# Row transposes of the next tile behind three products of the second gemm, beside those of the second relu half; the sum of the logits three products later

## The chip, the cores and the metric

One core of one Trainium2 chip runs the kernel. The metric is device time in microseconds (us). Before the change the median of three runs is 907.2 us (906.87 to 910.54).

## The reference

Causal attention with a retrieval memory (4 batches, 8 heads, 576 positions, width 64) gives 2304 token rows of 512 numbers. Two mixture-of-experts layers follow, 8 experts each, every token going to one expert only:

```python
logits = x @ w_gate                      # layer 1; layer 0 uses normalized rows
expert_idx = np.argmax(logits, axis=1)
for e in range(E):
    mask = expert_idx == e
    h = np.maximum(x[mask] @ w1[e], 0.0)      # 512 -> 1024
    out[mask] = gate_w[mask, None] * (h @ w2[e])   # 1024 -> 512
```

Everything is float32. The kernel keeps that precision by splitting each operand into a high and a low part (fp32r), so that each float32 product is three matrix products: high times high, high times low, low times high.

## The kernel before, in words

Up to about 270 us the attention runs, then layer 0 and layer 1. Tokens are sorted by expert into tiles of 128 rows. A layer is a row of tiles, `step(L, t)` (L1374), with t the tile's number in the layer. The change concerns t=1 to t=21 of both layers; t=0 has code of its own.

One tile on TensorE (PE): **gemm 0** makes two halves of the hidden activations, 12 products into `ph0` and 12 into `ph1`. Each half goes through a relu on ScalarE (ACT, L1392 and L1413), then four 128x128 transposes on PE into `pt0` or `pt1` (`hT`, L1362), then `hilo`: ACT copies the high part (L1193), VectorE (DVE) subtracts to give the low part (L1194). **gemm 1** makes 24 products into `py`, here called q0 to q23, three to each 128-deep block. q0 and q1 read the high part of the first half; q2 is the first product that reads its low part, and q12 the first that reads the second half. The first half's transposes stand among the products of `ph1`, the second half's between q2 and q3.

The rows of the next tile have been gathered by then (`xg`); four transposes (`xT_pe`, L1189) bring them into `psx`, and another `hilo` makes `b.x` of them. In layer 0, four small transposed products with the second layer's gate weights (`parts_pe`, L1292) are copied out by `parts_ev` (DVE, L1295), and one more product (`logits_pe`, L1299) adds the four parts up to the logits of the tile finished before. DVE then routes: `iov` (L1312), `mn`, `t8s`, `km`, `oh` (L1319 to L1323), later `ea`, `sg`, `xcb` (L1327 to L1332). The matrix `oh` feeds `rank_pe` (L1335) in the next tile.

Weights are shared by the tiles of one expert. Where a new expert is coming, each 128x1024 chunk of its weights is split by ACT (L922, high) and by DVE (L925, low); these stand behind runtime branches (`splits`, L1261) at fixed places of each tile, and run only in the tiles that need them: chunk 2 of gemm 0's weights (`splits(0, (2,))`) around the second half's `hilo`, chunk 3 behind the routing up to `oh`, the other chunks behind it and in the next tile. The words that hold the branch flags are loaded in `next_step`. Each engine works through its own queue in the order in which the code writes it, so the order of these lines is the order of the work.

Of the kernel before, what the change touches and what calls it, by code (L numbers as in the profile page):

```python
# [409 lines left out]
def tile_kernel(ctx, tc, q, k, v, M_prev, z_prev, beta, emb, tau, w1a, w2a, wg, w1b, w2b, out):  # L410
# [190 lines left out]
    def place(c0, n):  # L601
        for _ in place_(c0, n):
            pass

    class Route1:
# [32 lines left out]
        def rank_pe(self, ps):  # L638
            n, mm = self.n, nc.tensor.matmul
            self.ps = ps[:, 0:n * E].rearrange("p (n e) -> p n e", e=E)  # L640
            mm(ps[:, 0:n * E], tri, self.o.rearrange("p n e -> p (n e)"), start=True, stop=False)
            mm(self.ps, ones, acc.unsqueeze(1).to_broadcast([P, n, E]), start=False, stop=(n == 1))
            for i in range(n - 1):
                mm(self.ps[:, i + 1:], ones, self.o[:, i:i + 1].to_broadcast([P, n - 1 - i, E]), start=False, stop=(i == n - 2))
# [22 lines left out]
        def rank_ev(self):  # L667
            V = nc.vector
            V.tensor_tensor(out=self.t8, in0=self.o, in1=self.ps, op=ALU.mult)
            yield  # L670
            V.tensor_reduce(out=rkb[:, self.sl], in_=self.t8, axis=AX.X, op=ALU.add)
            yield
# [254 lines left out]
    def split_chunk(c, wv):  # L927
        return [split_hi(c, wv), split_lo(c, wv)]
# [7 lines left out]
    def cp(e, out, in_):  # L936
        if e:
            nc.scalar.activation(out=out, in_=in_, func=AF.Copy)
        else:
            nc.vector.tensor_copy(out, in_)  # L940

    class Hooks:
# [125 lines left out]
        def parts_pe(self, b, ps):  # L1068


            self.ps["lp"] = ps
            g = KD * E
            for n in range(KD):
                nc.tensor.matmul(ps[g * n:g * n + g], enT.rearrange("p k e -> p (k e)"), self.xT[b][:, n, 0:512], start=True, stop=True)

        def parts_ev(self, b):
            cp(1, self.xT[b][:, 0, 0:512], self.ps["lp"])
# [75 lines left out]
    def rows_of(t):  # L1153

        return xgt[t % 2] if t else xg0
# [5 lines left out]
    def drain(g):  # L1161
        for _ in g:
            pass
# [11 lines left out]
    psx, pm1, ph1, pt0, pt1, py, pm0, ph0 = (psp.tile([P, 512], F32, name=x) for x in ("psx", "pm1", "ph1", "pt0", "pt1", "py", "pm0", "ph0"))  # L1175
# [11 lines left out]
    def xT_pe(x):  # L1187
        for kk in range(KD):
            nc.tensor.transpose(psx[:, P * kk:P * kk + P], x[:, P * kk:P * kk + P], ident)  # L1189

    def hilo(ps, hl):
        hi, lo = hl
        nc.scalar.activation(out=hi, in_=ps, func=AF.Copy)  # L1193
        nc.vector.tensor_tensor(out=lo, in0=ps, in1=hi.bitcast(F32), op=ALU.subtract)  # L1194
# [91 lines left out]
    pts = (pt0, pt1)  # L1286
# [10 lines left out]
    def logits_pe(yT):  # L1297

        nc.tensor.matmul(pm1[:, 0:E], yT[:, 0:P], sel, start=True, stop=True)  # L1299

    def yT_pe():
        for kk in range(KD):
            nc.tensor.transpose(pm0[:, P * kk:P * kk + P], ysb[:, P * kk:P * kk + P], ident)

    def yT_ev(yT):
        nc.scalar.activation(out=yT, in_=pm0, func=AF.Copy)
# [4 lines left out]
    def route2_iov():  # L1311
        nc.vector.tensor_scalar(out=rs_["iov"], in0=ioer, scalar1=xcb[:, 2:3], scalar2=None, op0=ALU.mult)  # L1312
# [30 lines left out]
    def begin(L, t):  # L1343

        if t:
            nc.gpsimd.tensor_copy(xca[t % 2], rows_of(t)[:, DM:XR])  # L1346
        if 1 < t < NS - 2:
            gather(L, t + 2)

    def end(L, t):  # L1350
        xc = xca[t % 2] if t else xg0[:, DM:XR]
        nc.scalar.activation(out=ysb, in_=py, func=AF.Copy, scale=xc[:, 0:1])  # L1352
        if L == 0:
            nc.gpsimd.tensor_copy(xcb, xc)
            nc.gpsimd.dma_start(out=x2[P * t:P * t + P, 0:DM], in_=ysb)
        else:
            nc.gpsimd.indirect_dma_start(out=out, out_offset=bass.IndirectOffsetOnAxis(ap=xc[:, 1:2].bitcast(I32), axis=0), in_=ysb, in_offset=None,  # L1357
                                         bounds_check=NTOK - 1, oob_is_err=False)

    def hT(i, b):  # L1360
        for kk in range(4):
            nc.tensor.transpose(pts[i][:, P * kk:P * kk + P], b.hs[i][:, P * kk:P * kk + P], ident)  # L1362
        hilo(pts[i], b.h[i])

    def next_rows(t):
# [3 lines left out]
    def next_step(L, t):  # L1369
        n = steps[L, t] = Step(L, t)  # L1370
        if t > 2:
            n.flags()

    def step(L, t):  # L1374

        s, b = steps[L, t], bufs
        more = 0 < t < NS - 1
        split2 = t > 2
        rt2 = L == 0
        late = t >= NT1 - 2  # L1380
        x = x0 if t == 0 else b.x
        lx = lambda kk: (*x, P * kk)
        lh = lambda kk: (*b.h[kk // 4], P * (kk % 4))
        begin(L, t)
        s.gemm(0, ph0, lx, 0, 0, 3)
        yield
        s.gemm(0, ph0, lx, 0, 3, 9)
        yield
        s.gemm(0, ph0, lx, 0, 9, 12)
        if split2:  # L1390
            s.splits(0, (0, 1))
        nc.scalar.activation(out=b.hs[0], in_=ph0, func=AF.Relu)  # L1392
        if split2:
            s.splits(1, (0,))

        ahead = (L, t) != (0, NT1 - 1)
        if ahead and split2:
            s.loads(0, (0, 1))
            s.loads(1, (0,))
        yield  # L1400
        s.gemm(0, ph1, lx, 512, 0, 6)
        hT(0, b)
        if rt2:
            yT_pe()
            yT_ev(b.hs[0])
        yield
        rk = L == 0 and 2 <= t <= NT1 - 2
        if rk:
            rank_pe(t - 2)
            rank_ev(t - 2)  # L1410
        s.gemm(0, ph1, lx, 512, 6, 12)
        last_mm[0] = s.lm[1]
        nc.scalar.activation(out=b.hs[1], in_=ph1, func=AF.Relu)  # L1413
        yield
        if more:
            xT_pe(rows_of(t + 1))
        if rt2:
            parts_pe(b.hs[0])
            parts_ev(b.hs[0])
        if more:  # L1420
            hilo(psx, b.x)
        if rt2:
            route2_iov()
        s.gemm(1, py, lh, 0, 0, 3)
        if split2:
            s.splits(0, (2,), "h")
        hT(1, b)
        if split2:
            s.splits(0, (2,), "l")
        if more:  # L1430
            next_step(L, t + 1)
        yield
        s.gemm(1, py, lh, 0, 3, 6)
        cs = (1, 2, 3)
        if t == NE:
            s.splits(1, cs)
            cs = ()
        gen = iter(())
        if rt2:
            logits_pe(b.hs[0])  # L1440
        yield
        s.gemm(1, py, lh, 0, 6, 9)
        if rt2:
            gen = route2(t - 1)
        next(gen, None)
        next(gen, None)
        if split2:
            s.splits(0, (3,))
        if split2 and cs:
            s.splits(1, cs)  # L1450
        if t == 2:
            s.flags()
            s.splits(0, range(4))
            s.loads(0, range(4))
        if not ahead:
            e2.append(nc.values_load(ini[0:1, 1, 0:1], engines=[SP_], min_val=0, max_val=E - 1))
            s.loads(0, (0, 1))
            s.loads(1, (0,))
        if split2:
            s.loads(0, (2, 3))  # L1460
            s.loads(1, (1, 2, 3))
        drain(gen)
        if rk and ((t - 1) % 6 == 0 or t == NT1 - 2):
            c0 = (t - 2) // 6 * 6
            place(c0, t - 1 - c0)
        for q_ in range(9, 24, 3):
            yield
            s.gemm(1, py, lh, 0, q_, q_ + 3)
        last_mm[1] = s.lm[1]
        if (L, t) == (1, NT1 - 2):  # L1470

            nc.gpsimd.drain()
        if rt2:
            nc.gpsimd.dma_start(out=x2[P * (t - 1):P * t, DM:XR], in_=xcb)  # L1474
            if late:
                rank_pe(t - 1)
                rank_ev(t - 1)
                place(t - 1, 1)
        if not ahead:

            with tc.If(rg["nt"] <= NT1):
                for c in range(8):
                    for ins in split_chunk(c, rg["wv"]):
                        tc.add_to_no_dep_group("n18", ins)
        end(L, t)
# [71 lines left out]
    b = Bufs(lambda i: Wh[0][:, 1, 512 * i:512 * i + 512] if i < 6 else None)  # L1557
    s = steps[0, 0] = Step(0, 0)
    lx = lambda kk: (*b.x, P * kk)
    lh = lambda kk: (*b.h[kk // 4], P * (kk % 4))  # L1560
# [39 lines left out]
    nc.scalar.activation(out=b.hs[1], in_=ph1, func=AF.Relu)  # L1600
    lo(4)
    hT(0, b)
    hT(1, b)
    run(C, 5)
# [42 lines left out]
    s, b, c = steps[1, 0], bufs, NS - 1  # L1647
    lx = lambda kk: (*x0, P * kk)
    lh = lambda kk: (*b.h[kk // 4], P * (kk % 4))
# [105 lines left out]
```

## Time and profile before

| | before |
|---|---|
| runs, us | 910.54, 906.87, 907.2 (median 907.2) |
| profiled execution, us | 905.06 |
| its span, first to last instruction, us | 903.2 |
| mean granted TensorE clock | 0.991 |
| busy: PE, DVE, ACT, us | 870.2, 502.1, 483.8 |

The profiled execution is 2.1 us below the median of the runs. Times in the rows are counted from the start of its span.

### The profile page before, as it was taken

What the parts mean: (1) busy time and instruction counts of PE and PEld (TensorE: products, weight loads), DVE (VectorE), ACT (ScalarE), POOL (GpSimd) and SP (SyncE); (2) the same over time, 40 slices, a digit from 0 to 9 for tenths busy, and PEclk for the clock granted to TensorE, in tenths of its full rate; (3) what the DMA queues carried; (4) which work ended last, traced back from release to release, by engine and by line L of the source; (5) the groups of instructions that cost most, each with busy time, mean ns of one, the idle gap of its engine ahead of it and who ended that gap; (6) DMA issues with size and microseconds to landing.
All of it is one profiled execution on the core that took longest, in us unless ns stands there. A gap on an engine that the chain in (4) does not pass through costs nothing. (4 is left out here: it accounts for less than half of the span.)

```text
span 903.2 us, 20913 instructions
## 1 busy us (share of the span) xinstructions
PE 870.2 (96%) x5347; PEld 686.9 (76%) x5347; DVE 502.1 (56%) x1585; ACT 483.8 (54%) x972; POOL 275.3 (30%) x375
## 2 busy tenths in 40 slices
PE   6999999999989999998999999998999999999996
PEld 4777777677667777786888877886868888888885
DVE  4655656565684676379535666643567314463430
ACT  3657666666756735376435554532367435564531
POOL 5557635543633011212122312121231212321221
PEclk9999999999999999999999999998999999999998
DMA  7322352411333155359515317111668514384111
GB/s 130 80 52 82 73 170 78 101 40 41 100 111 113 59 211 175 108 165 314 177 49 164 108 37 235 38 49 40 234 203 297 171 48 139 130 305 135 43 38 39
DMA packets 102438, 110.32 MB, mean 122 GB/s; under 512 B 69882, under 2 KB 69882, under 8 KB 102276
## 3 DMA queue, kind: packets, MB, share of 16 engines
q1 hardware_dynamic: 94244, 85.33, 31.1%
q0 software_dynamic: 8032, 23.22, 7.8%
q8 instruction: 54, 0.88, 0.4%
q14 instruction: 108, 0.88, 0.3%
HBM read 90.32 MB, written 19.25 MB: 121 GB/s over the span
## 5 line engine op out<-in xcount | busy, mean ns | idle before, releaser
L1250 PE MATMUL py<-Wh,b 128*128 (+1 forms) x688 | 240.8, 406 | 2.6 <-DVE b L1194 2.4
L1250 PE MATMUL ph<-Wh,b 128*128 (+1 forms) x672 | 226.7, 398 | 0.5 <-ACTq L1261 0.5
L925 DVE TENSOR_TENSOR Wl<-stg,Wh 128x1024 f32 (+1 forms) x120 | 145.5, 1224 | 79.8 <-ACT Wh L922 74.4
L1250 PEld LDWEIGHTS py<-Wh,b 128*128 128x128 f32 x688 | 129.3, 188 | 32.6 <-issue 5.3
L1250 PEld LDWEIGHTS ph<-Wh,b 128*128 128x128 f32 x672 | 126.1, 188 | 26.7 <-ACTq L1261 0.9
L922 ACT ACTIVATE Wh<-stg 128x1024 f32 (+1 forms) x120 | 125.6, 1057 | 25.8 <-DVEq L1261 5.9
L1250 PE MATMUL py<-Wl,b 128*128 (+1 forms) x344 | 134.8, 392 | 0.0
L1250 PE MATMUL ph<-Wl,b 128*128 (+1 forms) x336 | 131.1, 390 | 2.7 <-DVEq L1261 2.7
L1194 DVE TENSOR_TENSOR b<-pt,b 128x512 fp32r<-128x512 f32 x86 | 59.4, 691 | 104.0 <-ACT b L1193 102.2
L287 ACT ACTIVATE att<-psat 128x512 f32<-128x512 f32 (+1 forms) x144 | 66.7, 463 | 70.6 <-PE psat L285 69.5
L308 PE MATMUL psav<-vb,att 128*128 128x128 f32 (+1 forms) x640 | 96.3, 281 | 2.9 <-ACT att L287 2.8
L308 PEld LDWEIGHTS psav<-vb,att 128*128 128x128 f32 x640 | 81.3, 191 | 17.3 <-ACT att L287 5.9
L1357 POOL DMA_INDIRECT out_dram<-ysb,xca x21 | 27.1, 1292 | 190.5 <-ACTq L1261 122.7
L1193 ACT ACTIVATE b<-pt 128x512 fp32r<-128x512 f32 x86 | 51.5, 598 | 62.9 <-PE pt L1362 61.4
L1250 PEld LDWEIGHTS ph<-Wl,b 128*128 128x128 f32 x336 | 63.2, 188 | 14.9 <-DVEq L1261 3.4
L1250 PEld LDWEIGHTS py<-Wl,b 128*128 128x128 f32 x344 | 64.9, 189 | 9.9
L233 DVE CUSTOM_DVE_ANT_0 a<-pss,wmask 128x128 f32<-128x128 f32 (+3 forms) x128 | 61.0, 485 | 19.2 <-PE pss L255 11.0
L268 ACT ACTIVATE a<-a,mx 128x128 f32<-128x128 f32 (+3 forms) x128 | 71.2, 556 | 0.4 <-DVE mx L233 0.3
L1352 ACT ACTIVATE ysb<-py,xca 128x512 f32<-128x512 f32 x42 | 28.8, 686 | 76.5 <-PE py L1250 65.8
L1159 POOL DMA_INDIRECT xg<-x_scratch,idx x48 | 55.6, 1157 | 38.4 <-issue 14.9
L1474 POOL DMA_DIRECT2D x_scratch<-xcb x21 | 11.9, 566 | 162.1 <-DVE xcb L1332 59.4
L285 PE MATMUL psat<-ident,a 128*128 128x128 f32 x320 | 56.9, 276 | 1.0 <-ACT a L268 0.8
(380 smaller groups left out, 1280.4 us busy)
## 6 DMA issues: line engine op xcount, KB each, us to landing
stg<-in_moe_w_dram SPq DMA_DIRECT2D x120, 512.0 KB
x_scratch<-ysb POOLq DMA_DIRECT2D x22, 256.0 KB
qkn<-in_q_dram SPq DMA_DIRECT2D x32, 128.0 KB
qkn<-in_k_dram SPq DMA_DIRECT2D x32, 128.0 KB
vb<-in_v_dram SPq DMA_DIRECT2D x32, 128.0 KB
x_scratch<-xb SPq DMA_DIRECT2D x16, 256.0 KB
x_scratch<-stg SPq DMA_DIRECT2D x11, 258.0 KB
xg<-x_scratch,idx POOLq DMA_INDIRECT x48
```

Of the source, the lines that this page charges most:

```text
L233: nc.vector.tensor_tensor_reduce(out=out, in0=ps, in1=mask, scale=1.0, scalar=bound, op0=ALU.add, op1=ALU.min, accum_out=m)
L268: nc.scalar.activation(out=a[:, 0:N], in_=a[:, 0:N], func=AF.Exp, scale=-1.0, bias=mx, accum_out=rs_t[pi][:, c, j:j + 1])
L285: nc.tensor.transpose(ps[:, 128 * i:128 * i + 128], x, ident)
L287: nc.scalar.activation(out=att[:, 0:N], in_=ps[:, 0:N], func=AF.Copy)
L308: nc.tensor.matmul(av_t[pi][:, c, j:], att[:, 128 * kb:128 * kb + 128], vn[:, kb, j:, 0:D], start=(kb == 0), stop=(kb == c))
L922: return nc.scalar.activation(out=chunk(Wh, c, wv), in_=stg[:, c].unsqueeze(1), func=AF.Copy).ins
L925: return nc.vector.tensor_tensor(out=chunk(Wl, c, wv), in0=stg[:, c].unsqueeze(1), in1=chunk(Wh, c, wv).bitcast(F32), op=ALU.subtract).ins
L1159: return nc.gpsimd.indirect_dma_start(out=rows_of(t), out_offset=None, in_=rows, in_offset=bass.IndirectOffsetOnAxis(ap=idx[:, L, t:t + 1] ...
L1193: nc.scalar.activation(out=hi, in_=ps, func=AF.Copy)
L1194: nc.vector.tensor_tensor(out=lo, in0=ps, in1=hi.bitcast(F32), op=ALU.subtract)
L1250: mm = nc.tensor.matmul(ps, x[:, col:col + P], W, start=(first and q_ == qs[0]), stop=(last and q_ == qs[-1]))
L1352: nc.scalar.activation(out=ysb, in_=py, func=AF.Copy, scale=xc[:, 0:1])
```

## The change

In every tile with t from 1 to 21 the products q0 to q2 move ahead of the next tile's row transposes. These now stand directly before the second half's transposes, and in layer 0 `parts_pe` directly behind both. On ACT and DVE the second half's `hilo` comes before the copy of the parts, the `hilo` of the next rows and `iov`. In layer 0 the logits product stands behind q8, no longer behind q5, and chunk 3's split ahead of `mn` to `oh`. Transposes, products and copies are the same in number and shape.

```diff
--- before.py
+++ after.py
@@ -1357,9 +1357,12 @@
             nc.gpsimd.indirect_dma_start(out=out, out_offset=bass.IndirectOffsetOnAxis(ap=xc[:, 1:2].bitcast(I32), axis=0), in_=ysb, in_offset=None,
                                          bounds_check=NTOK - 1, oob_is_err=False)
 
-    def hT(i, b):
+    def hT_pe(i, b):
         for kk in range(4):
             nc.tensor.transpose(pts[i][:, P * kk:P * kk + P], b.hs[i][:, P * kk:P * kk + P], ident)
+
+    def hT(i, b):
+        hT_pe(i, b)
         hilo(pts[i], b.h[i])
 
     def next_rows(t):
@@ -1412,19 +1415,22 @@
         last_mm[0] = s.lm[1]
         nc.scalar.activation(out=b.hs[1], in_=ph1, func=AF.Relu)
         yield
+        s.gemm(1, py, lh, 0, 0, 3)
+        if split2:
+            s.splits(0, (2,), "h")
+
         if more:
             xT_pe(rows_of(t + 1))
+        hT_pe(1, b)
         if rt2:
             parts_pe(b.hs[0])
+        hilo(pts[1], b.h[1])
+        if rt2:
             parts_ev(b.hs[0])
         if more:
             hilo(psx, b.x)
         if rt2:
             route2_iov()
-        s.gemm(1, py, lh, 0, 0, 3)
-        if split2:
-            s.splits(0, (2,), "h")
-        hT(1, b)
         if split2:
             s.splits(0, (2,), "l")
         if more:
@@ -1436,16 +1442,16 @@
             s.splits(1, cs)
             cs = ()
         gen = iter(())
+        yield
+        s.gemm(1, py, lh, 0, 6, 9)
         if rt2:
             logits_pe(b.hs[0])
-        yield
-        s.gemm(1, py, lh, 0, 6, 9)
+        if split2:
+            s.splits(0, (3,))
         if rt2:
             gen = route2(t - 1)
         next(gen, None)
         next(gen, None)
-        if split2:
-            s.splits(0, (3,))
         if split2 and cs:
             s.splits(1, cs)
         if t == 2:
```

PE, middle of a tile of layer 0 (`b_4235` and `b_4236` are high and low part of the first half, `hs_4229` the second relu half), before:

```order
L1189 MATMUL psx<-ident,xg_4231 128x128 x4
L1292 MATMUL pm_4146<-hs_4228,wgT 32x128 x4
L1250 MATMUL py<-Wh_4134,b_4235 128x512
L1250 MATMUL py<-Wl_4136,b_4235 128x512
L1250 MATMUL py<-Wh_4134,b_4236 128x512
L1362 MATMUL pt_4144<-ident,hs_4229 128x128 x4
L1250 MATMUL py<-Wh_4134,b_4235 128x512
L1250 MATMUL py<-Wl_4136,b_4235 128x512
L1250 MATMUL py<-Wh_4134,b_4236 128x512
L1299 MATMUL pm_4141<-sel,hs_4228 128x8
```

and after, from q2 on:

```order
L1250 MATMUL py<-Wh_4134,b_4236 128x512
L1189 MATMUL psx<-ident,xg_4231 128x128 x4
L1362 MATMUL pt_4144<-ident,hs_4229 128x128 x4
L1292 MATMUL pm_4146<-hs_4228,wgT 32x128 x4
L1250 MATMUL py<-Wh_4134,b_4235 128x512
L1250 MATMUL py<-Wl_4136,b_4235 128x512
L1250 MATMUL py<-Wh_4134,b_4236 128x512
L1250 MATMUL py<-Wh_4134,b_4235 128x512
L1250 MATMUL py<-Wl_4136,b_4235 128x512
L1250 MATMUL py<-Wh_4134,b_4236 128x512
L1299 MATMUL pm_4141<-sel,hs_4228 128x8
```

The row transposes stood ahead of q0; they now stand behind q2, and with them the parts. The logits stand behind six products that follow the parts and not behind three.

DVE, middle of a tile of layer 0 (`b_4238` is the second half's low part, `b_4234` that of the next rows), before:

```order
L1341 TENSOR_TENSOR acc<-acc,oh 128x8
L1295 COPY hs_4228<-pm_4146 128x128
L1194 TENSOR_TENSOR b_4234<-psx,b_4233 128x512
L1312 TENSOR_SCALAR iov<-ioer,xcb 128x8
L1261 COMPARE_AND_BRANCH
L1261 UNCONDITIONAL_BRANCH x2
L1194 TENSOR_TENSOR b_4238<-pt_4144,b_4237 128x512
L1261 COMPARE_AND_BRANCH
L925 ISA x2
L925 TENSOR_TENSOR Wl_4135<-stg,Wh_4133 128x1024
L1261 UNCONDITIONAL_BRANCH x2
```

and after:

```order
L1339 SCALAR_TENSOR_TENSOR rj,rkb<-pm_4141,oh 128x8
L1341 TENSOR_TENSOR acc<-acc,oh 128x8
L1261 COMPARE_AND_BRANCH
L1261 UNCONDITIONAL_BRANCH x2
L1194 TENSOR_TENSOR b_4238<-pt_4144,b_4237 128x512
L1295 COPY hs_4228<-pm_4146 128x128
L1194 TENSOR_TENSOR b_4234<-psx,b_4233 128x512
L1312 TENSOR_SCALAR iov<-ioer,xcb 128x8
L1261 COMPARE_AND_BRANCH
L925 ISA x2
L925 TENSOR_TENSOR Wl_4135<-stg,Wh_4133 128x1024
L1261 UNCONDITIONAL_BRANCH x2
```

The second half's low part moved ahead of the copy of the parts, the next rows' low part and `iov`. These three now stand between it and the split of chunk 2.

DVE, layer 0, t=3, where the three chunks of gemm 1's weights are split early; difference from before to after:

```order
 L925 TENSOR_TENSOR Wl_4136<-stg,Wh_4134 128x1024 x3
 L1261 UNCONDITIONAL_BRANCH x2
+L1261 COMPARE_AND_BRANCH
+L925 TENSOR_TENSOR Wl_4135<-stg,Wh_4133 128x1024
+L1261 UNCONDITIONAL_BRANCH x2
+L1277 UNCONDITIONAL_BRANCH x2
 L1319 TENSOR_REDUCE mn<-pm_4141 128x1
 L1320 SCALAR_TENSOR_TENSOR t8s<-pm_4141,mn,iov 128x8
 L1322 TENSOR_REDUCE km_4155<-t8s 128x1
 L1323 TENSOR_SCALAR oh<-t8s,km_4155,xcb 128x8
-L1261 COMPARE_AND_BRANCH
-L925 TENSOR_TENSOR Wl_4135<-stg,Wh_4133 128x1024
```

The split of chunk 3 moved ahead of the routing's four operations.

## Rows read from the trace of the kernel before

**Rows 1.** The page, part 1: busy time of TensorE, share of the span, count.

```profile
PE 870.2 (96%) x5347; PEld 686.9 (76%) x5347; DVE 502.1 (56%) x1585; ACT 483.8 (54%) x972; POOL 275.3 (30%) x375
```

**Rows 2.** Timeline of PE, layer 0, t=11 (start, us, engine, line, operation [idle <-releaser]).

```profile
464.54 0.40 PE L1250 MATMUL ph<-Wh,b 128*128 x1
464.78 0.60 PE L1189 MATMUL psx<-ident,xg 128*128 128x128 f32 x4
...
465.67 0.50 PE L1250 MATMUL py<-Wh,b 128*128 x1
...
466.46 0.60 PE L1362 MATMUL pt<-ident,hs 128*128 128x128 f32 x4
466.82 0.48 PE L1250 MATMUL py<-Wh,b 128*128 x1
...
467.60 0.28 PE L1299 MATMUL pm<-sel,hs 128*128 128x8 f32 x2
```

**Rows 3.** Timeline of PE, layer 0, t=19: eight transposes side by side.

```profile
574.06 0.60 PE L1362 MATMUL pt<-ident,hs 128*128 128x128 f32 x4
574.49 0.60 PE L1303 MATMUL pm<-ident,ysb 128*128 128x128 f32 x4
574.85 0.48 PE L1250 MATMUL ph<-Wh,b 128*128 x1
```

**Rows 4.** Timeline of PE, layer 0, t=7 and t=8.

```profile
409.83 0.50 PE L1250 MATMUL py<-Wh,b 128*128 x1 [0.90 <-DVE b L1194]
410.17 0.60 PE L1362 MATMUL pt<-ident,hs 128*128 128x128 f32 x4
...
425.19 0.50 PE L1250 MATMUL py<-Wh,b 128*128 x1 [1.46 <-DVE b L1194]
```

**Rows 5.** Timeline of PE and of DVE, layer 0, t=6, around the second relu half.

```profile
395.36 0.60 PE L1362 MATMUL pt<-ident,hs 128*128 128x128 f32 x4
...
394.80 0.29 DVE L1295 COPY hs<-pm 128x128 f32<-128x128 f32 x1 [1.02 <-PE pm L1292]
...
395.61 0.22 DVE L1312 TENSOR_SCALAR iov<-ioer,xcb 128x8 f32<-128x8 f32 x1
396.62 0.69 DVE L1194 TENSOR_TENSOR b<-pt,b 128x512 fp32r<-128x512 f32 x1 [0.79 <-ACT b L1193]
```

**Rows 6.** Windows: stretch, length, busy PE, PEld, DVE, ACT, POOL, clock, DMA share, GB/s.

```profile
397.20:409.80 12.60, 11.73 (x65) 9.21 (x63) 11.81 (x23) 11.38 (x15) 0.56 (x1) 1.00 0.75 243
```

**Rows 7.** Timeline of DVE and of PE, layer 0, t=3 into t=4.

```profile
361.00 0.16 DVE L1319 TENSOR_REDUCE mn<-pm 128x1 f32<-128x8 f32 x1
...
362.06 0.50 PE L1250 MATMUL ph<-Wl,b 128*128 x1 [1.43 <-DVEq L1261]
```

**Rows 8.** Timeline of PE and of DVE, layer 0, t=1.

```profile
322.34 0.40 PE L1250 MATMUL ph<-Wh,b 128*128 128x512 f32 x1
...
322.78 0.69 DVE L1194 TENSOR_TENSOR b<-pt,b 128x512 fp32r<-128x512 f32 x1
...
326.42 0.18 DVE L837 TENSOR_TENSOR idx<-fx,pm 128x25 int32<-128x25 f32 x1
```

**Rows 9.** Timeline of ACT and of PE, layer 1, t=3 into t=4.

```profile
669.04 3.24 ACT L922 ACTIVATE Wh<-stg 128x1024 f32 x3 [1.77 <-DVEq L1261]
...
672.38 0.49 PE L1250 MATMUL ph<-Wh,b 128*128 x1 [0.51 <-ACTq L1261]
674.11 0.50 PE L1250 MATMUL ph<-Wl,b 128*128 x1 [1.23 <-DVEq L1261]
```

**Rows 10.** Timeline of PE and of DVE, layer 1, t=5 and t=6.

```profile
692.02 0.39 PE L1250 MATMUL ph<-Wh,b 128*128 x1
...
692.31 0.69 DVE L1194 TENSOR_TENSOR b<-pt,b 128x512 fp32r<-128x512 f32 x1 [0.17 <-DVEq L1261]
...
704.32 0.39 PE L1250 MATMUL ph<-Wh,b 128*128 x1
...
704.34 0.68 DVE L1194 TENSOR_TENSOR b<-pt,b 128x512 fp32r<-128x512 f32 x1
```

## The prediction

> **What bounds the kernel now.** I read the page's busy times first: TensorE (PE) is busy 870.2 of 903.2 us, 96% [rows 1]. So a time is won or lost here only where PE does less work, runs work at a worse place, or waits. Then the timeline of PE gave what each piece of the tile's middle takes, and the idle times in it gave the few waits that there are. Last, I followed those waits into the timelines of VectorE (DVE) and ScalarE (ACT).
>
> I call e the start of the last product of gemm 0. In a steady tile of layer 0 [rows 2] e is 464.54, the row transposes start 0.24 later, q0 at 1.13, the second half's transposes at 1.92, q3 at 2.28, the logits at 3.06. Products follow each other about every 0.23 us (464.54 to the transposes that follow: 0.24). Nothing waits there.
>
> **What the change does to PE's own work.** Nothing is taken away. The question is whether two runs of transposes cost less when joined. Alone, four transposes stand 0.36 us ahead of the next product (466.46 to 466.82 [rows 2]), and the three products from there to the logits take 0.78 and not 3 x 0.23, so a site costs 0.36 + 0.09 = 0.45. Eight side by side are in the trace already, at the first half's transposes and those of the last result [rows 3]: 574.06 to 574.85 is 0.79, and with the same 0.09 behind 0.88. Two sites alone make 0.90. So joining is worth 0.01 to 0.02 us per tile, over 42 tiles 0.4 to 0.8; I take **-0.4**. The logits cost the same behind q8 as behind q5.
>
> **What moves: q2 comes early.** In before, the row transposes (and in layer 0 the parts) stood ahead of q0: useful work during which DVE finished the low part of the first half, which q2 reads. Now q2 is the third product behind e, due at e + 0.68. Where it must wait, the row in which it does so [rows 4] shows the price: the low part is ready, q2 starts 0.05 later (at 409.83), and the next transposes follow 0.34 after that (410.17), where 0.24 is usual. So the transposes start at the low part's end + 0.39, against e + 0.92 without a wait: a tile loses what the low part's end exceeds e + 0.53. In most tiles it ends earlier than that and costs nothing. The exceptions are the tiles in which DVE splits weights just ahead of it.
>
> The Trainium skill, TensorE: Matmul & The Clock Gate, "Step-by-step: what each phase is for", says that weight loads are pulled ahead of running products, while the products themselves stay in program order. The second half of this is what makes the row transposes useless as cover once they stand behind q2. By its first half the load of q2 would hide and the 0.10 would be saved, some 1 us less over ten tiles; the rows with the wait show that it was not saved there.
>
> *Layer 1, steady split tiles.* At t=6 the low part starts at 704.34 and takes 0.68, e is 704.32: it ends at e + 0.70, a loss of 0.17 [rows 10]. Six tiles read alike (t=4, 6, 11, 13, 15, 18): 6 x 0.17 = **+1.05**; if the load of q2 hid, 0.07 each, 0.4. At t=5 it ends at 692.31 + 0.69 = 693.00, e + 0.98 [rows 10], a loss of 0.45; t=14 is its twin. Both have a DVE that is busy without a break since the tile before, so they also inherit that DVE's delay (worked out next, here 0.4, of which PE is itself 0.17 late): 2 x (0.45 + 0.23) = **+1.35**, at least 0.8.
>
> *Layer 0, t=7 and t=8.* Here q2 already waits, 0.90 and 1.46 us [rows 4], and DVE works without a longer break before both: 11.81 of the 12.60 us ahead of t=7's low part are busy, 23 instructions, the rest lies between them [rows 6]. Two things add up.
> First, the row transposes and parts (464.54 to 465.67 is 1.13 in place of 0.23, and the restart is 0.11 slower: 1.01 us [rows 2]) were done ahead of the wait; they now come behind it. Each of the two tiles is 1.01 longer.
> Second, DVE starts its splits later. Before, the parts' copy, the next rows' low part and `iov` filled time in which DVE waited for the second half anyway: from 394.80 to 395.83 they take 1.03, and 0.79 of idle follows [rows 5]. Now they come behind the second half's low part and ahead of the split. That low part itself comes earlier, since its transposes start at e + 0.92 + 0.44 = e + 1.36 and not e + 1.92, so the split of t=6 is 1.03 - 0.56 = 0.47 late, and through the unbroken DVE so is q2 of t=7. At t=7 the transposes follow q2's wait at + 0.34 + 0.44 and not + 0.34, so the split is 0.47 + 0.44 + 1.03 = 1.94 late, and q2 of t=8 with it. Behind q2 of t=8 come its own 1.01: **+2.95**. At t=9 the low part would be some 0.45 later against e; no long run of splits stands ahead of it, so I let it end there. If DVE's delay were all absorbed, 2.0 would be left; that is the low end.
>
> *Layer 0, t=1.* e is 322.34, the low part ends at 322.78 + 0.69 = 323.47 [rows 8], e + 1.13: 0.60 lost. The logits moreover write the bank that DVE still reads for `idx`, and with 1.03 of copies ahead of it that read ends about 1.0 later than at 326.60 [rows 8], while the logits, three products later, are due at about 327.2: 0.4 more. **+1.0**, and between 0.6 and 1.15.
>
> *Layer 1, t=3.* ACT's three splits (669.04) wait for DVE and for the words that stand behind both hilos; q0 and q1 of the next tile wait for ACT and DVE, 0.51 and 1.23 us [rows 9]. Those words now stand behind the next rows' hilo as well, one copy of 0.60 and one of 0.69 with 0.3 of waiting: the splits and so the next tile's start come about 0.93 later, which contains the 0.44 that PE has more to do behind its own wait. **+0.93**, between 0.44 and 1.04.
>
> **What is gained.** Layer 0, t=3: PE stands still for 1.43 us in t=4 until DVE has passed the branch of chunk 3, and ahead of this branch stand `mn` to `oh`, from 361.00; PE goes on at 362.06 [rows 7]. With the branch first, 0.95 of the 1.06 go, and the second half's low part no longer stands behind `iov` there, which waits for GpSimd: up to 0.3 more. **-1.2**, between -0.95 and -1.3. `oh` is later for it, but its reader is the rank product in the middle of the next tile.
>
> **Costed at nothing, and its cover.** The logits now wait for the parts' copy, which stands behind the second half's low part. DVE takes up the second half's low part 1.26 behind the start of its transposes (395.36 to 396.62 [rows 5]), here at e + 2.62, and passes on some 0.61 later to the copy of 0.29, out at e + 3.53; the logits are due at e + 2.25 + 0.78 + 0.68 = e + 3.7. The load of their weights comes a product earlier, so the slack is some 0.03 to 0.15 us. If that cover is gone, each of about 18 tiles of layer 0 loses up to 0.1: 0 to +1.8, taken as 0. The second relu's transposes come 0.56 earlier; in layer 0 the 0.60 between q2's due time and them is left to it, and nothing in the rows waits for it now.
>
> **Sum.** -0.4 + 1.05 + 1.35 + 2.95 + 1.0 + 0.93 - 1.2 = **+5.7 us**. On the profiled execution's own 905.06 that is 910.8. The median of the runs is 907.2, 2.1 above it; I put the difference on the median: **912.9 us**, +0.6%. The lower ends make -0.8 + 0.4 + 0.8 + 2.0 + 0.6 + 0.44 - 1.3 = +2.1, the upper ends, with the logits, 0 + 1.05 + 1.4 + 2.95 + 1.15 + 1.04 - 0.95 + 1.8 = +8.4.
>
> **Rivals.** About 0.5%, 4.5 us, is what a measurement of this kernel can tell from no change.
>
> *The delays do not carry.* One place decides: whether DVE at t=7 and t=8, and at t=5 and t=14 of layer 1, takes its start from the second half's low part or from the splits' high parts on ACT. If ACT's chain is what paces it, q2 waits where it did, and only the moved work (2 x 1.01) and the small waits remain, less the gain at t=4: the low sum, +2.1, 909.3 us, not slower by this measure. For it: ACT is busy 11.38 of 12.60 us there [rows 6]. Against it: the idle time named at q2 and in DVE's rows is DVE's own. It decides at a DVE shift of under 0.2. Chance 0.32.
>
> *The logits become a wait.* With 0.1 per tile of layer 0 the sum is +7.5, 914.7 us. For it: a slack near nothing. Against: both ends come from rows without any waiting. Inside the slower cases, 0.15 of them all.
>
> *Joining is worth more than the rows show.* A run of twelve transposes and parts might lose the whole restart, 0.09 to 0.11 per tile: 42 x 0.1 = 4.2, with the gain at t=4 5.4, less the low stalls of 4.2: 906.0. It takes stalls at nothing as well to be faster by 0.5%. Against it: rows 3 are such a joined run and keep the restart. Chance 0.06, of which 0.05 is put to faster.
>
> That the change does not do what it says is excluded by the order of the built instructions.
>
> **How the numbers follow.** Slower by over 0.5%: 0.58, the sum with its upper ends and the logits. Within 0.5%: 0.37, the low sum and the sums up to +4.5. Faster: 0.05. The range takes the low case with a further us for the place of the median among its runs, and the upper ends: 907.5 to 916.0.
>
> **What would show it.** Waits of PE at q2, named for the low part on DVE, at t=1, 7 and 8 of layer 0 (about 0.5, 2 and 3 us, longer than before) and at eight tiles of layer 1; PE's wait in t=4 of layer 0 down from 1.43 to 0.3; the first products of layer 1's t=4 waiting at least as long as before; steady tiles equal to within 0.03. I am wrong if q2 shows no waits beyond t=7 and t=8, or if a steady tile gets shorter by 0.1.

## The result, and the profile after

Over 13 runs each, the median went from 905.67 to 912.79 us; the ratio is 1.007, 95% interval 1.005 to 1.009. The profiled execution of after has a span of 914.3 us against 903.2 before. The kernel is slower by more than its own scatter, by 6 to 7 us.

The page's part 1 (busy us, share of the span, instructions) shows the same number of instructions on each engine as [rows 1] and a TensorE (PE) that is "busy" longer:

```profile
PE 877.5 (96%) x5347; PEld 692.1 (76%) x5347; DVE 497.9 (54%) x1585; ACT 484.9 (53%) x972; POOL 272.1 (30%) x375
```

First the steady tile, the timeline of PE in layer 0, t=11 (start, us, engine, line, operation, [idle <-releaser]). It answers to [rows 2]:

```profile
470.58 0.40 PE L1250 MATMUL ph<-Wh,b 128*128 x1
470.81 0.39 PE L1250 MATMUL py<-Wh,b 128*128 x1
...
471.27 0.40 PE L1250 MATMUL py<-Wh,b 128*128 x1
471.50 0.60 PE L1189 MATMUL psx<-ident,xg 128*128 128x128 f32 x4
471.94 0.60 PE L1362 MATMUL pt<-ident,hs 128*128 128x128 f32 x4
472.47 0.42 PE L1292 MATMUL pm<-hs,wgT 128*32 128x128 f32 x8
472.83 0.50 PE L1250 MATMUL py<-Wh,b 128*128 x1
...
474.34 0.28 PE L1299 MATMUL pm<-sel,hs 128*128 128x8 f32 x2
```

With e = 470.58: q2 at e + 0.69, the transposes at 0.92 and 1.36, q3 at 2.25, the logits at 3.76, each within 0.06 of where the prediction put it, and PE waits nowhere. From the first product of a tile to the first of the next, such a tile took 13.63 to 13.65 us before and takes 13.64 to 13.67 now, a tile of layer 1 without splits 12.28 to 12.30 and 12.29 to 12.30. So joining the transposes brought nothing, and putting the logits later cost nothing.

The time went to a few tiles. The waits of PE in layer 0, t=1, t=4, t=7 and t=8 (timeline of PE; before in [rows 4, 7, 8]):

```profile
325.43 0.50 PE L1250 MATMUL py<-Wh,b 128*128 128x512 f32 x1 [0.28 <-DVE b L1194]
...
363.63 0.50 PE L1250 MATMUL ph<-Wl,b 128*128 x1 [0.15 <-DVEq L1261]
...
412.24 0.75 PE L1250 MATMUL py<-Wh,b 128*128 x1 [2.37 <-DVE b L1194]
412.79 1.05 PE L1189 MATMUL psx<-ident,xg 128*128 128x128 f32 x4
413.64 1.06 PE L1362 MATMUL pt<-ident,hs 128*128 128x128 f32 x4
414.63 0.66 PE L1292 MATMUL pm<-hs,wgT 128*32 128x128 f32 x8
415.22 0.73 PE L1250 MATMUL py<-Wh,b 128*128 x1
...
430.18 0.50 PE L1250 MATMUL py<-Wh,b 128*128 x1 [2.49 <-DVE b L1194]
430.52 0.60 PE L1189 MATMUL psx<-ident,xg 128*128 128x128 f32 x4
```

At t=7 and t=8 q2 waits for the low part of the first half on DVE, 2.37 and 2.49 us instead of 0.90 and 1.46, and the transposes now stand behind it. At t=7 there is something more: four transposes, 0.44 apart from the next group elsewhere (430.52 to 430.96 at t=8), take 0.85 there. The windows of after (stretch, length, busy PE, PEld, DVE, ACT, POOL, granted clock, DMA share, GB/s) give the reason, and the same in layer 1, t=4:

```profile
412.00:416.00 4.00, 3.76 (x19) 2.77 (x20) 0.98 (x6) 1.18 (x3) 1.94 (x4) 0.57 0.99 364
416.00:420.00 4.00, 4.00 (x20) 3.32 (x19) 3.81 (x9) 3.94 (x4) 0.00 (x0) 1.00 0.50 146
...
430.00:434.00 4.00, 3.82 (x27) 3.04 (x28) 2.06 (x9) 2.15 (x3) 1.44 (x3) 1.00 0.94 311
...
680.00:684.00 4.00, 2.69 (x8) 2.12 (x9) 2.68 (x3) 2.11 (x2) 3.52 (x3) 0.75 0.82 273
684.00:688.00 4.00, 4.00 (x18) 3.27 (x17) 1.61 (x2) 2.00 (x3) 0.52 (x1) 0.83 0.99 325
```

Behind the wait of t=7 PE was granted a clock of 0.57, and behind those of layer 1, t=4, of 0.75 and 0.83, on the mean of each stretch: part of the time half of its full 2.4 GHz. Behind the wait of t=8 it stayed at 1.00. In layer 1, t=4 (timeline of PE, before in [rows 9]) the products stand 0.43 apart and not 0.23 until 685.2:

```profile
679.06 0.51 PE L1250 MATMUL ph<-Wh,b 128*128 x1 [0.92 <-ACTq L1261]
681.31 0.50 PE L1250 MATMUL ph<-Wl,b 128*128 x1 [1.74 <-DVEq L1261]
681.64 0.76 PE L1250 MATMUL ph<-Wh,b 128*128 x2
682.21 0.63 PE L1250 MATMUL ph<-Wl,b 128*128 x1
682.63 1.05 PE L1250 MATMUL ph<-Wh,b 128*128 x2
683.49 0.63 PE L1250 MATMUL ph<-Wl,b 128*128 x1
```

Tile by tile (first product to first product of the next tile, after less before, each from one profiled execution), with what the prediction had:

| tiles | predicted | after - before |
|---|---|---|
| layer 0, t=1 and 2 | +1.0 | +1.08 - 0.13 |
| layer 0, t=4 | -1.2 | -0.96 |
| layer 0, t=7 and 8 | +2.95 | +3.01 + 1.04 |
| layer 1, t=3 and 4 | +0.93, and 0.17 of the six tiles | +0.42 + 2.26 |
| layer 1, t=5 and 14 | +1.35 | +0.57 + 0.61 |
| layer 1, t=6, 11, 13, 15, 18 | 0.17 each | +0.19, 0.18, 0.17, 0.02, 0.19 |
| layer 0, t=16 to 21, with the change of layers | 0 | +1.36 - 1.21 |
| all others | -0.4 | about +0.2 |

The sum, from the first tile of layer 0 to the end, is +9.0 us in this pair of executions. The rest of the 11.1 us between the two spans lies before the first tile, in the attention, whose code is the same. The pair shows more than the medians do: the profiled execution of after is the longest of its 13, 915.98 us at a mean granted clock of 0.989, where the five shortest (909.42 to 911.9) had 0.994 or 0.995.

### The profile page after: what moved, and what is told of

The parts are those of the page before. It is cut to its first block, busy times and chain, and to the rows that moved or that the text cites. A ratio compares the mean times of both kernels' runs of the same rounds, so it can differ in the third digit from the quotient of the medians.

```text
span 914.3 us, 20884 instructions
## 1 busy us (share of the span) xinstructions
PE 877.5 (96%) x5347; PEld 692.1 (76%) x5347; DVE 497.9 (54%) x1585; ACT 484.9 (53%) x972; POOL 272.1 (30%) x375
## 5 line engine op out<-in xcount | busy, mean ns | idle before, releaser
L1193 ACT ACTIVATE b<-pt 128x512 fp32r<-128x512 f32 x86 | 51.4, 598 | 75.1 <-PE pt L1362 65.2
L1357 POOL DMA_INDIRECT out_dram<-ysb,xca x21 | 24.1, 1148 | 196.0 <-ACTq L1261 125.7
```

## The experiments

Layers, copies and order refer to `step`. The pieces of code show the calls that a run moves or adds, with the conditions around them and the switches that choose an order left out; "..." stands for lines between. The runs were made in three batches; each ratio is against runs of the kernel before in the same batch.

**One layer at a time.** In the first, layer 1 keeps the old order; in the second, layer 0.

```diff
+        if L == 0:      # second run: if L == 1
             s.gemm(1, py, lh, 0, 0, 3)
             xT_pe(rows_of(t + 1))
             hT_pe(1, b)
...
+        else:
+            xT_pe(rows_of(t + 1))
...
```

> The change in layer 0 alone, layer 1 in the old order. Theory (TensorE waits at q2, and moved work that no longer covers them): the waits at t=1, 7 and 8 less the gain at t=4, and behind the longest wait a stretch at half clock; by the tiles of the two profiles about +4 us on before. Rival (the cost is spread over all tiles, some 0.15 us each): +3.1 and tiles longer by 0.1 to 0.2 without any wait.

Measured: 911.15 us, ratio 1.0056 (1.0034 to 1.0078). Layer 0's tiles read as in after: t=1 +1.12, t=4 -1.06, t=7 +2.97, t=8 +2.06, steady tiles 0.01 to 0.03 longer.

> The change in layer 1 alone. Theory: no layer 0 gain or loss; t=3 into t=4 longer by 0.9 to 2.7 us (the latter with a fall of the clock behind the wait), t=5 and t=14 by 0.6 each, six tiles by 0.17, others equal: +3 to +5 us. Rival (spread over all tiles): tiles without splits longer too.

Measured: 911.2 us, ratio 1.0062 (1.0040 to 1.0084): t=3 and 4 +0.67 and +1.97, t=5 +0.60, t=14 +0.61, t=6, 11, 13 and 18 +0.15 to 0.18, steady tiles equal. Both times the loss is where the waits are and not spread; that rival falls. But by their ratios the two parts, 5.1 and 5.6 us, make more than the whole's 6.3, each with some 2 us of interval to either side. The clock accounts for most of that, by an estimate: its mean over the nine runs is 0.9892 and 0.9894, over before's in this batch 0.9915, over after's 0.9911. If all the clock that was not granted was time lost, 0.0022 of 910 us is some 2 us in each of the two, and 3.1 and 3.7 are left. The first run's profile shows one place where it fell: layer 1, t=4, is longer by 1.58 there, though layer 1 is in the old order. It waits 0.52 and 1.23, as in [rows 9], and then the clock falls (windows, columns as above):

```profile
676.00:680.00 4.00, 2.26 (x8) 1.23 (x7) 2.64 (x3) 2.81 (x4) 1.61 (x3) 0.86 0.60 194
680.00:684.00 4.00, 4.00 (x14) 3.22 (x13) 2.26 (x2) 1.70 (x3) 1.90 (x1) 0.71 0.95 330
```

In the profiled execution of before the same waits were followed by 1.00. So whether the clock falls behind a wait of this size differs from execution to execution, of the old order too, and one pair of profiles can be some 1.5 us off for each such place.

**Is it the standing still that the clock falls behind?** PE gets something to do during the three long waits.

```diff
+    if L == 0 and t in (7, 8):     # between q1 and q2
+        for _ in range(4):
+            xT_pe(rows_of(t))
+    if (L, t) == (1, 4):           # between q0 and q1 of gemm 0
+        for _ in range(4):
+            xT_pe(rows_of(t))
```

> After, with 16 further transposes of rows already at hand (their result is not used) put into the wait ahead of q2 at t=7 and t=8 of layer 0 and between q0 and q1 of t=4 of layer 1. Theory (TensorE standing still for some 2.4 us is what the fall of the clock follows): the granted clock stays at 1.00 behind these places, the products there keep their 0.23 us, and the kernel with more work is up to 3 us faster than after, about 910. Rival (the fall has another cause, or transposes do not hold the clock): the clock falls to 0.5 to 0.6 as in after, 913 or more.

Measured: 944.64 us, ratio 1.0421 (1.0390 to 1.0452). This failed as an experiment: the rows were not at hand. Their buffer is already being filled again by the gather for a later tile, and PE waited for that (timeline of PE):

```profile
421.14 3.25 PE L1189 MATMUL psx<-ident,xg 128*128 128x128 f32 x14 [8.30 <-DMA xg<-x_scratch,idx]
```

So it was made again with an operand that never changes, the identity:

```diff
-            xT_pe(rows_of(t))
+            for kk in range(KD):
+                nc.tensor.transpose(psx[:, P * kk:P * kk + P], ident, ident)
```

> After, with 16 transposes of the identity (their result is not used, their operand is at hand from the start) put ahead of q2 at t=7 and t=8 of layer 0 and between q0 and q1 of t=4 of layer 1. Theory (the clock falls after TensorE stood still for over 2 us): the granted clock stays at 1.00 behind these places, and with 48 more transposes the kernel is 1.4 to 3 us faster than after, about 910. Rival (the fall has another cause, or transposes do not hold the clock): 0.5 to 0.6 behind the waits as in after, 912 or more.

Measured: 911.16 us, ratio 1.0056 (1.0036 to 1.0075), against 1.007 (1.005 to 1.009) for after: the runs alone do not separate the two. The profile does. Timeline of PE at t=7 (in this kernel the added transposes are L1193, the products L1254, the second half's transposes L1366), and windows of 4 us behind t=7's wait and around t=4 of layer 1:

```profile
409.43 1.91 PE L1193 MATMUL psx<-ident 128*128 128x128 f32 x16
411.98 0.50 PE L1254 MATMUL py<-Wh,b 128*128 x1 [0.65 <-DVE b L1198]
412.32 0.60 PE L1189 MATMUL psx<-ident,xg 128*128 128x128 f32 x4
412.76 0.60 PE L1366 MATMUL pt<-ident,hs 128*128 128x128 f32 x4
```

```profile
412.00:416.00 4.00, 4.00 (x28) 3.20 (x29) 2.06 (x8) 2.52 (x4) 1.93 (x4) 1.00 1.00 351
416.00:420.00 4.00, 4.00 (x19) 3.30 (x19) 3.71 (x7) 3.83 (x6) 0.00 (x0) 1.00 0.80 245
676.00:680.00 4.00, 3.08 (x22) 2.31 (x20) 3.63 (x3) 2.29 (x4) 1.18 (x1) 1.00 0.36 122
680.00:684.00 4.00, 4.00 (x18) 3.24 (x19) 2.45 (x2) 3.25 (x4) 2.87 (x3) 1.00 0.94 326
```

The clock stays at 1.00 behind all three places. t=7 and t=8 are now longer than before by 1.47 and 1.51, where the prediction's working, which has no change of clock, gives 1.48 and 1.47; layer 1, t=4, by 0.67 and not 2.26. The 16 transposes cost nothing where they fill a wait: at t=7 and t=8 q2 still waits behind them (0.65 and 1.23), and at t=4 of layer 1 the product behind them comes 2.24 behind the one ahead, as in after. That transposes held the clock fits this, but it is one execution, and at t=8 the clock had stayed at 1.00 in after too. All the runs point the same way: the mean granted clock is 0.9928 over 12 runs with the transposes, 0.9911 over 13 of after, 0.9909 over 28 of before in this batch.

**Is it the place of q2?** The first product that reads a low part is moved behind the transposes.

```diff
-        s.gemm(1, py, lh, 0, 0, 3)
+        s.mms(1, py, lh, 0, (0, 1, 3), True)
         xT_pe(rows_of(t + 1))
         hT_pe(1, b)
...
-        s.gemm(1, py, lh, 0, 3, 6)
+        s.mms(1, py, lh, 0, (4, 2, 5))
```

> After, with the products of gemm 1 in another order: q0, q1, q3 ahead of the transposes and q4, q2, q5 behind them (q8 behind q10 too), so that the first product with the first half's low part comes sixth and behind the transposes. Theory (the place of q2 is the cause): waits at q2 vanish but for 0.2 to 0.5 at t=7 and 8, no fall of the clock in layer 0, 5 to 6 us less than after, about 907. Rival (delay of the copies on ScalarE and VectorE is the cause): no more than 2 us less.

Measured: 905.74 us, ratio 0.9992 (0.9971 to 1.0012): the whole loss is gone, with everything else of the change in place. (q2 is the fifth product in this order, not the sixth.) t=7 and t=8 are shorter than before by 0.42 and 0.52, the tiles of layer 1 that had lost 0.17 or 0.6 are within 0.03 of before. The rival (the copies' delay) allowed 2 us less; it was 7. So the loss comes about at q2. The run does not say how much of it is moved work and how much the copies' delay, since a later q2 hides both; and this order of products is a gain in before's order as well (t=7 there 0.82 shorter, in the better version below), so part of what it gives here is its own. Layer 1, t=4, is still 2.10 longer, by its waits for the splits and the clock behind them.

**The gain alone.**

```diff
+        if split2:
+            s.splits(0, (3,))
         if rt2:
             gen = route2(t - 1)
...
-        if split2:
-            s.splits(0, (3,))
```

> Before, with only the split of chunk 3 put ahead of the routing in layer 0. Theory: the wait of 1.43 us in t=4 of layer 0 falls to about 0.4, all other tiles as before: -1.0, 904.5. Rival (the wait moves to the next engine): no change in t=4.

Measured: 906.97 us, ratio 0.9994 (0.9977 to 1.0012). No gain to be seen, though the interval does not exclude the 1.0 us that was expected. The wait in t=4 fell from 1.43 to 0.75 only, and t=3 became 0.49 longer by a wait at q14, the first product that reads the second half's low part:

```profile
355.13 0.73 PE L1250 MATMUL py<-Wh,b 128*128 128x512 f32 x2 [0.20 <-DVEq L1261]
...
360.70 0.50 PE L1250 MATMUL ph<-Wl,b 128*128 x1 [0.75 <-DVEq L1261]
```

DVE's timeline shows why: the second half's low part still stands behind `iov`, which waits for GpSimd's copy of `xcb`, and that waits for a transfer.

```profile
353.94 0.18 POOL L1354 COPY xcb<-xca 128x4 f32<-128x4 f32 x1 [5.57 <-DMA x_scratch<-xcb]
354.16 0.23 DVE L1312 TENSOR_SCALAR iov<-ioer,xcb 128x8 f32<-128x8 f32 x1 [2.29 <-POOL xcb L1354]
354.38 0.69 DVE L1194 TENSOR_TENSOR b<-pt,b 128x512 fp32r<-128x512 f32 x1
```

In after it stands ahead, and the transfer does not matter to it. But in this execution the copy of `xcb` came 10.56 us behind the start of t=3, the latest in the twelve profiles (8.56 to 10.56; 9.88 in before). Those 0.68 go through to the splits, whose first starts 2.02 behind the low part's end here and 2.03 in before. By an estimate from these rows, with the copy where before had it, q14 would not wait and the wait in t=4 would be some 0.1. In the better version below the low part stands behind `iov` too, with the copy at 9.55 and the flag words loaded later, and the wait in t=4 is gone. So it is not shown that the gain at t=4 needs both moves.

**DVE's delay alone, and the cover of the logits.** TensorE's transposes in the old place, only the copies in the new order; first with the logits behind q5, then behind q8.

```diff
         xT_pe(rows_of(t + 1))
         parts_pe(b.hs[0])
-        parts_ev(b.hs[0])
-        hilo(psx, b.x)
-        route2_iov()
         s.gemm(1, py, lh, 0, 0, 3)
         hT_pe(1, b)
         hilo(pts[1], b.h[1])
+        parts_ev(b.hs[0])
+        hilo(psx, b.x)
+        route2_iov()
```

> TensorE in the old order, and only ScalarE's and VectorE's copies in the new one (second half ahead of parts, next rows and iov), split of chunk 3 in its old place. Theory (VectorE's later splits carry over): q2 waits some 1.0 longer at t=7 and t=8 of layer 0 each, t=4 of layer 1 starts 0.9 later, t=5 and t=14 show waits of up to 0.3: +3 us, 908.5, more where a longer wait brings the clock down. Rival (the delays are absorbed): the tiles of before, 905.5.

Measured: 930.99 us, ratio 1.0273 (1.0250 to 1.0297). I had overlooked that the logits then wait for the parts' copy in 19 tiles of layer 0, by 0.92 (the waits of PE in layer 0: engine, line, cause, us in total, times, longest):

```profile
PE pm L1299 <- DVE hs L1295: 17.4, 19, 0.9
PE py L1250 <- DVE b L1194: 1.8, 2, 1.2
```

> As the run with only ScalarE's and VectorE's copies in the new order, but the logits behind q8, so that they stand clear of the parts' copy. TensorE's transposes where they were before. Theory (VectorE's later splits carry over): steady tiles as before; q2 waits longer by 1.0 at t=7, and t=8 is longer by about 1.0 too; in layer 1 the start of t=4 later by 0.9, t=5 and t=14 longer by 0.2 to 0.4: +3 us, 909. Rival (the later splits are absorbed): the tiles of before.

Measured: 922.68 us, ratio 1.0175 (1.0147 to 1.0204). Three products later, the logits still wait, 0.22 each, and the steady tile is 0.50 longer:

```profile
PE pm L1299 <- DVE hs L1295: 4.0, 18, 0.2
PE py L1250 <- DVE b L1194: 2.7, 2, 1.6
```

With the second half's transposes 0.56 earlier, as in after, that wait is gone. After's steady tile, t=11, shows how narrowly: the parts' copy ends at 474.09, and the load of the logits' weights starts at 474.15, 0.08 later than it could have by the trace; the logits behind it do not wait:

```profile
473.81 0.28 DVE L1295 COPY hs<-pm 128x128 f32<-128x128 f32 x1
474.15 0.38 PEld L1299 LDWEIGHTS pm<-sel,hs 128*128 128x128 f32 x2
```

These two runs answer the question on DVE's delay only in part, since TensorE itself is later in each tile. q2's waits grew from 2.4 to 2.7 us on top of the 0.5 of each tile ahead, which is a delay that carries and not one that is absorbed. Layer 1, free of logits, shows t=14 longer by 0.43 and t=5 by 0.16. In both runs, t=21 of layer 0 was some 3.8 us longer, for a reason that I did not follow; the first tile of layer 1 gave 2.8 and 1.6 of that back.

**A better version.** Before's order, with three edits: the low part's first product behind the second half's transposes, chunk 3's split ahead of the routing in layer 0, and at t=3 the flag words loaded behind the splits of gemm 1's weights.

```diff
-        s.gemm(1, py, lh, 0, 0, 3)
+        s.mms(1, py, lh, 0, (0, 1, 3), True)
         hT(1, b)
-        if more:
+        if more and t != NE:
             next_step(L, t + 1)
-        s.gemm(1, py, lh, 0, 3, 6)
+        s.mms(1, py, lh, 0, (4, 2, 5))
         if t == NE:
             s.splits(1, cs)
+            if more:
+                next_step(L, t + 1)
```

> An attempt at a better version: before's order of TensorE and of the copies; products q0, q1, q3, transposes of the second half, q4, q2, q5 (low part of the first half later); chunk 3 split ahead of the routing in layer 0; at t=3 of both layers the words for the next tiles loaded behind the splits of gemm 1's weights and not ahead. Theory: the waits at t=7 and 8 of layer 0 (0.90 and 1.46) shrink by 0.9 each at least, those at the start of t=4 of both layers (1.43, and 0.51 with 1.23) go, and the fall of the clock behind the latter too: -4 to -6 us, about 900.5. Rival (weights arriving set these times, not their splits): within 1.5 us of before.

Measured: 900.38 us, ratio 0.9942 (0.9923 to 0.9961), faster than both kernels. Layer 0, t=4, is 1.73 shorter than before, t=7 0.82, t=8 0.50, layer 1, t=3 and 4, 0.66 and 0.59. The 0.9 that were expected at t=7 and 8 each were not reached, and the waits ahead of t=4 of layer 1 shrank and did not go. Of the waits that this aimed at, these are left in layer 0 and in layer 1:

```profile
PE py L1250 <- DVE b L1194: 0.4, 1, 0.4
...
PE ph L1250 <- DVEq L1261: 0.7, 1, 0.7
PE ph L1250 <- ACTq L1261: 0.4, 1, 0.4
```

> The better version with q2 one product later still (q0, q1, q3, transposes of the second half, q4, q6, q2, q7, q5). Theory: the wait of 0.4 that is left at t=8 of layer 0 falls by 0.2, all else equal: 0 to 0.3 us under the version before it, about 900.

Measured: 898.71 us, ratio 0.9923 (0.9898 to 0.9948). The intervals of the two overlap; t=8 was 0.43 longer than in the version before it and not shorter, so this last shift is not shown to be worth anything.

## Why the prediction was right

The forecast, 912.9 us, lies 0.1 from the median of 912.79. That closeness is partly luck: it was put on a median of before of 907.2, which over more runs is 905.1 to 906.6, and the ratio asks for +6.3, not +5.7. The terms tell more.

*What bounds the kernel.* Right. PE did the same work, and only its waits, and the clock behind some of them, moved the time.

*Joining the transposes.* The sign was off by a little: -0.4 forecast, and steady tiles up to 0.04 longer. The reading of [rows 3], that a joined run saves no more than 0.02 a tile, held; so the rival that joining is worth 0.1 a tile is out.

*q2 comes early.* Right in mechanism and price. The rule "the low part's end + 0.39" gave 0.17 for [rows 10]; four of the five tiles at t=6, 11, 13, 15 and 18 lost 0.17 to 0.19. (Six times 0.17 is 1.02; the prediction wrote 1.05.) t=15 lost 0.02: in before its q3 already came 0.34 later than in the other tiles (7.74 us behind the tile's start, 7.40 at t=13), for a reason that the trace does not name, and it comes at 7.74 in after too. t=5 and t=14 lost 0.57 and 0.61, against 0.68 each: the low part ends at e + 1.11 and e + 1.14, so the rule gives 0.58 and 0.61, and what was put too high is DVE's delay, 0.13 and 0.18 and not 0.23. The run with q2 behind the transposes took the whole loss away. The signs came in part: a wait at q2 shows at t=1, 7 and 8 of layer 0 (0.28, 2.37 and 2.49), but in layer 1 only at t=3, 5 and 14 (0.50, 0.31 and 0.34); the tiles that lost 0.17 show the loss and no wait in the timeline.

*t=7 and t=8.* The term was +2.95, measured +4.05 in after, and +2.98 where PE was kept at work during the waits. In that run the parts can be read one by one. q2 of t=7 comes 9.50 us behind the tile's start and not 8.99, 0.51 later (forecast 0.47); q2 of t=8, counted from the start of t=7, 2.02 later (forecast 1.94); and 0.97 come behind it (forecast 1.01). So moved work and DVE's delay were sized right, DVE's delay carries, and the bound of 2.0 for an absorbed delay is out. What the pair of profiles has beyond it is the clock, 1.07 us over both tiles, for which the sum had no term.

*t=1.* +1.0 against +0.95, in the two parts that it was made of: q3 comes 0.56 later (forecast 0.60), and the logits stand until `idx` is read, which is 0.5 more (forecast 0.4).

*Layer 1, t=3.* +0.93, with 0.17 of t=4 itself 1.1; measured +2.68, and +1.09 with PE kept at work. The two waits grew from 0.51 and 1.23 to 0.92 and 1.74, by 0.92 in all. The rest is again the clock, 1.6 us.

*The gain at t=4.* -1.2 against -0.96. The wait at the branch gave what it should: the products on its two sides start 0.54 apart (0.31 more than without a wait) and no longer 1.82, so 1.28 are saved. But a new wait took 0.3 back, which the prediction had missed. ScalarE's `th` now waits for a `t8s` that stands behind the split, the result's copy and the first relu are queued behind `th`, and the first half's transposes wait for that relu: they start 0.47 behind the product ahead of them, where 0.23 is usual. ScalarE and PE there:

```profile
364.14 0.27 ACT L1325 ACTIVATE th<-pm,mn 128x8 f32<-128x8 f32 x1 [3.31 <-DVE t8s L1320]
364.31 0.68 ACT L1352 ACTIVATE ysb<-py,xca 128x512 f32<-128x512 f32 x1
365.17 0.60 ACT L1395 ACTIVATE hs<-ph 128x512 f32<-128x512 f32 x1 [0.18 <-ACTq L1261]
...
365.82 0.66 PE L1362 MATMUL pt<-ident,hs 128*128 128x128 f32 x4
```

*Costed at nothing.* The logits' slack held, narrowly: their weights' load waits 0.08 for the parts' copy, they themselves do not, and 18 tiles wait 0.22 as soon as the transposes are 0.56 later. What the prediction did not see at all is t=18 of layer 0, 0.78 longer: its first transposes wait 0.54 and not 0.26 for ScalarE, and the rank product at its end comes later. It goes with the place of chunk 3's split: the run that moves this alone has t=18 longer by 0.65, and the run with layer 0 in the old order has t=17 and 18 together longer by 0.08. So by these profiles the new place that gains at t=4 costs some 0.5 there. The first tile of layer 1 gave 1.2 of all this back.

*The clock.* The sum has no term for it, and the profiled pair shows 2.7 us of it (1.07 and 1.6). Over all the runs little of that is left: the mean granted clock is 0.9911 in after and 0.9909 to 0.9915 in the three batches of before, whose executions lose clock too. With PE kept at work the tiles add up to +6.3, the ratio of the medians gives +6.3, and the forecast had +5.7. So the sum was right in its waits; that the clock could be left out was luck, since nothing in the prediction weighed it.

## What to carry to other kernels

Work that fills the time until an operand is ready is worth up to its own length there. Moving it behind the consumer cost nearly all of it in the tiles where the consumer waited already (0.97 of 1.01 us), and a part where the operand had come just in time and no wait was to be seen before (0.17 in tiles of layer 1). Price such a move from the row in which the consumer already waits, then follow the delay through the engine that makes the operand as far as that engine works without a break. Where a wait can't be removed, put the consumer later among its peers (here high products ahead of low ones) before moving anything else.

## What I had not expected of the hardware

TensorE's clock. Behind a wait of 2.37 us (layer 0, t=7) the granted clock was 0.57 over the next 4 us, its lower level for most of them, and the tile about 1.5 us longer than at the full clock; behind 2.49 at t=8 of the same execution it stayed at 1.00. With layer 0 alone changed it fell behind 2.37 at t=7 and behind 1.99 at t=8. Behind 0.52 and 1.23 us with one product between, it fell in one execution of layer 1's old order (0.71) and stayed at 1.00 in another. So the length of a wait did not decide it in these rows, and what does is left open. With 16 transposes of the identity in the wait it stayed at 1.00 at each of the three places, in the one execution that was profiled; over 12 runs the mean granted clock was 0.9928, against 0.9911 without them.
